# Background conversions of a fused attention and two-layer kernel: other places for the w_out halves, another order of the jobs, and earlier first sums

## The chip, the cores and the metric

The kernel runs on one core of a Trainium2 chip. The metric is the device time of one execution in microseconds (us). Engines are named as the profile names them: PE is TensorE (matmuls; PEld its weight loads), DVE is VectorE, ACT is ScalarE, POOL is GpSimd, SP is SyncE, which here only issues DMAs. Each engine works through its own queue in order and waits on semaphores for the others and for DMAs.

## The reference

What is computed, cut to what matters:

```
# attention: B=4, H=8, S=576, D=64; heads 0-3 local (32 back), 4-7 strided (every 32nd)
x  = softmax(mask(q @ k.T / 8)) @ v        # -> (2304 tokens, 512)
# layer 1
h  = x @ w_in1                             # (2304, 2048)
g  = s * relu(h)**2 + b
y  = g @ w_out1                            # (2304, 512)
# layer 2
h  = y @ w_in2
out = (h * cos(h)) @ w_out2
```

The weights reach the core as float64 words. They are turned into float32 on the chip.

## The kernel before, in words

**Arithmetic.** A float32 matmul is made of three fast ones: each operand is split into a high part (`split_hi`, L162, a copy on ACT into the type fp32r) and a low part (`split_lo`, L165, a subtraction on DVE), and PE forms hi·hi, lo·hi and hi·lo. `xhi` and `xlo` hold the activations, `gh` and `gl` those between w_in and w_out.

**Stages.** Attention comes first (until about 140 us, with slots beside it). Then, and partly beside it, come 40 *slots* (L881): one token block of up to 512 by one 128-wide slice of the hidden width, 30 slots for the first six slices, ten for two more. Slot 0 starts early; the last ends at 265.4 us. Then come 36 *units* (L1934): each does a pair of slices for 768 tokens with seven products of 2x2 blocks in place of eight, which need sums of blocks as operands, `xt`, `xdiff` (`run_forms1`, L1122) and sums of weight blocks. In a unit the products go to two banks `pa` and `pb`; ACT copies some out (`q<-pa`, L1946) and DVE adds a bank and a `q` into `h` (L1914). PE can write a bank again only after that. The w_out products of a unit (`triples`, L1814 and L1824) fill in between. Layer 2 begins at about 465 us, and its last part (`Blocks`, L1503 and L1633) at about 607 us.

**Background conversions.** While PE works through slots and units, the weights of the units to come are loaded, converted, split and stored in memory, and loaded again when the unit needs them (`wfl<-wfb`, `w2l<-w2s`). Such a job is a generator of single steps. A *pair* job (`pair_ops`): load 512 KB `praw` (L342), convert in place `ta` (L170 on ACT; L178, L179, L182 on DVE), four small sums `ts` (L355), three high splits (ACT), three low splits (DVE) into tiles `ob` and `oa`, three stores `wfb` (512 KB, L388), `wfa` (256 KB, L389), `wfc` (128 KB, L390). A *w_out* job (`out_ops`): load `oraw` (L395), convert in `tw` or in the spare end of q's tile, split into `ow`, store `w2s` (512 KB, L420). `ob`, `oa` and `ow` share the pool tag "v" with two places, so each new tile waits until the store of the tile two before has landed. `raw` tiles have two places as well.

**What sets the order.** The list `jobs2` gives the order of jobs: both halves of a pair, then both w_out tiles of it. How many steps go between two groups of matmuls stands in the tables `BG2` (by slot) and `BG2_UNIT` (by unit): a rate is added at each group, and whole steps are issued. So the steps stand at fixed points among the instructions of ACT, DVE and SP, and a step that waits holds what stands behind it on its engine. The conversion tiles come from pool "hs" (three places) up to slot 30, after it from "st" (four places). `run_forms1(0)` is started at slot 35 (`last == -5`) and gives one of its steps at each tick.

Of the kernel before, what the change touches and what calls it, by code (L numbers as in the profile page):

```python
# [9 lines left out]
F32 = mybir.dt.float32  # L10
F32R = mybir.dt.float32r
BF16 = mybir.dt.bfloat16
U32 = mybir.dt.uint32
AF = mybir.ActivationFunctionType
ALU = mybir.AluOpType
# [5 lines left out]
P = 128  # L21
# [7 lines left out]
KT = 64  # L29
LG, LK = 64, 96  # L30
# [50 lines left out]
HT = 384  # L81
# [25 lines left out]
LAST_USE = {"P2": 0, "P5": 1, "P3": 2, "P4": 3}  # L107
UNIT0 = ["P1", "P2", "t", "P6", "P5", "P7", "P3", "P4"]
UNIT = ["P1", "P2", "P6", "P5", "P7", "t", "P3", "P4"]
BG2 = ((15, 1.2), (18, 2.2), (22, 1.0), (30, 1.6), (36, 0.6), (38, 1.2))  # L110
BG2_UNIT = (1.2, 2.0, 2.0, 1.4, 1.4, 1.5, 1.5, 1.4, 1.6, 1.7, 1.7, 1.7, 1.4, 1.4, 1.4, 1.4, 1.4, 1.4, 1.4, 1.4, 1.6, 1.6)
NSUM = 6
ROOM = {10: (0, 2), 11: (0, 2), 12: (0, 2), 19: (1, 0), 20: (1, 1), 21: (0, 2), 22: (0, 2), 23: (1, 2), 24: (1, 1), 25: (0, 2), 26: (0, 2)}
OPERANDS = [(0, 0), (0, 1), (3, 1)]
MPLACES = [(5, 0), (4, 1)]
FORM_STEPS = (0, 0, 0, 3, 1, 1, 1, 3, 1, 1, 1, 3)
FORM_PACE = 4
TRIPLES = 12
TRIPLE_LAG = 2
LOADS = {  # L120
# [9 lines left out]
def net(ctx, tc, qkl, qks, rqk, vloc, vstr, rv, wi1, wo1, wp1, wo2, wp2, s, b, out):  # L130
    nc = tc.nc
# [16 lines left out]
    def psum(tag, name):  # L148
        return ps.tile([P, 512], F32, tag=tag, name=name, bufs={"h": 1, "acc": 4, "att": 3}[tag])

    ident = const.tile([P, P], F32, name="ident")
    identb = const.tile([P, P], BF16, name="identb")
    mloc = const.tile([P, 4, LK], BF16, name="mloc")
    mrem = const.tile([P, 4, KT], BF16, name="mrem")
    sb = const.tile([P, 32], F32, name="sb")
    xhi = const.tile([P, NC, NT], F32R, name="xhi")
    xlo = const.tile([P, NC, NT], F32R, name="xlo")
# [158 lines left out]
    def conv_tile(name):  # L316
        if plain_done[0]:
            return st_p.tile([P, 512], F32, tag="st", name=name)
        return h_p.tile([P, 512], F32, tag="hs", name=name)
# [76 lines left out]
        return raw  # L396

    def out_ops(raw, ly, n):
        t = whole = q0_tile()[:, HT:] if ly and n % 2 == 0 else conv_tile("tw")
        yield from to_f32(t, raw)  # L400
        bg2_load()
        if late:
            os = late_out(n % 2)
            t = t.rearrange("p (x c) -> p x c", x=2)
        else:
            o = io_p.tile([P, 2, 512], F32R, tag="v", name="ow")
            os = [o[:, h, :] for h in range(2)]
        apart = bool(late)
        yield lambda: split_hi(os[0], t)
        yield lambda: nc.sync.dma_start(out=w2f[n // 2][:, n % 2, :], in_=whole) if ly else None  # L410
        yield lambda: split_lo(os[1], t, os[0])
        yield lambda: None
        if apart:
            yield lambda: None
            for h in range(2):
                yield lambda h=h: nc.sync.dma_start(
                    out=w2s[ly, n][:, h, :].rearrange("p (x c) -> p x c", x=2), in_=os[h].bitcast(F32)
                )
        else:
            yield lambda: nc.sync.dma_start(out=w2s[ly, n], in_=o.bitcast(F32))  # L420
        stored2.add(("out", ly, n))

    def sum_load(p):
# [28 lines left out]

    jobs2 = []
    for ly, p in [(0, p) for p in range(PAIR1, NPAIR)] + [(1, p) for p in range(NPAIR)]:
        for m in range(2):
            jobs2.append((pair_load, pair_ops, (ly, p, m)))
        for f in range(2):
            jobs2.append((out_load, out_ops, (ly, 2 * p + f)))
    jobs2 += [(sum_load, sum_ops, (p,)) for p in range(NSUM)]
    gp = []  # L460
    loaded2 = []
# [2 lines left out]
    def q0_tile():  # L464
        if not qtile:
            qtile.append(rem_p.tile([P, HT + 512], F32, tag="rq", name="q0"))
        return qtile[0]
# [540 lines left out]
    early = 0  # L1008
# [116 lines left out]
    def new_temp(early):  # L1125
        return Temp(h_p.tile([P, 2, HT], F32, tag="hs", name="xt") if early else None)

    def split_temp(key, t):
        yield from free(key)
        hi, lo = place[key]  # L1130
        for m, src in t.ms:
            split_hi(hi[:, m], src)
        yield
        for m, src in t.ms:
            split_lo(lo[:, m], src, hi[:, m])
        formed.add(key)
        yield

    def run_forms1(s_):

        x11, x21, x12, x22 = (
            [x.bitcast(F32) for x in x_at(2 * s_ + half, kh)] for half in range(2) for kh in range(2)
        )
        key = {j: (0, s_, j) for j in range(2, 6)}
        early = s_ == 0
        t1, t2 = region_temps() if s_ == 2 else (new_temp(early), new_temp(early))
        yield from t1.set(x12[0], x12[1], ALU.add)
        for x in x11:
            yield from t1.set(t1, x)
        yield from t2.set(x22[0], t1)  # L1150
        yield from t2.set(t2, x22[1], ALU.add)
        if s_ < 2:
            yield from split_temp(key[3], t1)
        t4 = new_temp(early)
        yield from t4.set(x21[0], t2)
        yield from t4.set(t4, x21[1], ALU.add)
        yield from split_temp(key[2], t2)
        if s_ == 2:
            yield from split_temp(key[5], t4)
        for x in x11:  # L1160
            yield from t2.set(t2, x)
        if s_ == 2:
            yield from split_temp(key[3], t1)
        yield from split_temp(key[4], t2)
        if s_ < 2:
            yield from split_temp(key[5], t4)
# [140 lines left out]
    def region_temps():  # L1307
        return [Temp(x) for x in two(part_p.tile([P, RG], F32, tag="r21", name="xtemp"))]

    for t in range(NSLOT):  # L1310
        if t in W_AT:
            bg.append(lambda m=W_AT[t]: w_job(*m))
        for blk, need in ((1, 1), (2, 2), (3, 3)):
            if t == blk * FP:
                while not att.batch_done(need):
                    next(steps, None)
                    tick()
        last = t - NSLOT
        if t == 30:
            plain_done[0] = True  # L1320
        if last == -18:
            with tc.issue_after(relu[0].ins):
                nc.scalar.activation(sb[:, 4:5], sb[:, 3:4], AF.Sin)
        if last == -5:
            stages.append(run_forms1(0))
        if last == -3:
            spill(2)
        if last == -2:
            claim(2)
        if last == -1:  # L1330
            spill(1)
        for o, i in ((-9, 0), (-7, 1), (-5, 2), (-3, 3), (-2, 4), (-1, 5)):
            if last == o:
                load_wf(i)
        for o, i in ((-9, 0), (-8, 1), (-4, 2)):
            if last == o:
                load_w2(BUFS[i])
        first = t < FP
        for c in range(8):
            if c < 4 and (t, c) not in ((0, 0), (0, 1)):  # L1340
                mm_h(t, c)
            if c >= 4 and t >= LAG:
                mm_2(t - LAG, c - 4)
            tick()
            if c == 3:
                spawn(run_act(t))
            if c < 4 or t >= LAG:
                attention(RATE[min(t // FP, 2)])
            bg_step(BG0 if first or W_AT_FROM <= t < W_AT_TO else BG)
            for at, rate in BG2[::-1]:  # L1350
                if t >= at:
                    bg2_step(rate)
                    break
# [714 lines left out]
```

## Time and profile before

| | |
|---|---|
| median of 3 runs | 835.51 us (835.07 to 835.54) |
| the profiled execution | 833.12 us, span 831.3 us |
| PE busy | 817.1 us, 98% |
| DVE busy | 677.7 us, 82% |
| ACT busy | 585.5 us, 70% |
| granted TensorE clock | 1.00 (the 2.4 GHz level) |
| DMA | 220 MB, mean 265 GB/s |

The span is the time from the first to the last instruction of the profile; the execution's own time is 1.8 us longer. The profiled execution is 2.4 us below the median of the timed ones. PE is the engine to look at: where it stands idle, the time grows.

### The profile page before, as it was taken

The numbers are of one execution on the slowest core, as the hardware profiler recorded it, in microseconds if no ns is written. First come the engines' busy times: TensorE is split into PE (matmuls) and PEld (weight loads), VectorE is DVE, ScalarE is ACT, GpSimd is POOL, SyncE is SP. The second block draws the span as 40 slices with busy tenths as digits, with TensorE's granted clock in tenths as the row PEclk, the third lists the DMA queues.
The fourth block names the chain that finished last, engine by engine and source line by source line (L and its number), as shares of the span: only waits on it lengthen the run. The fifth ranks groups of instructions, "written<-read, shape, count | busy, mean of one in ns | idle before, by whom it ended". The sixth has DMA issues, their size and how long they took to land.

```text
span 831.3 us, 15491 instructions
## 1 busy us (share of the span) xinstructions
PE 817.1 (98%) x5545; PEld 731.7 (88%) x5545; DVE 677.7 (82%) x1294; ACT 585.5 (70%) x1232; POOL 20.5 (2%) x73
## 2 busy tenths in 40 slices
PE   8999999999999999999999999999999999999998
PEld 5677788788988899989989998899899999999998
DVE  6999665787998879996977698877758999578985
ACT  7888867768876787677678566557558765489753
POOL 3111000000000000000000000000000000000000
PEclk9999999999999999999999999999999999999999
DMA  9765433366989988887799989999798778874675
GB/s 338 237 190 166 135 105 92 122 248 227 324 318 343 366 324 285 313 290 267 264 346 371 295 281 345 318 311 383 255 358 264 269 249 253 290 259 152 205 250 179
DMA packets 101981, 220.00 MB, mean 265 GB/s; under 512 B 9104, under 2 KB 53392, under 8 KB 101904
## 3 DMA queue, kind: packets, MB, share of 16 engines
q1 hardware_dynamic: 100176, 211.83, 74.8%
q10 hardware_dynamic: 1728, 7.18, 2.4%
q8 instruction: 44, 0.72, 0.3%
q14 instruction: 33, 0.27, 0.1%
HBM read 163.92 MB, written 55.05 MB: 263 GB/s over the span
## 4 chain that ended last, share of the span: by engine, by line
PE 73%; DVE 13%; ACT 6%; DMA 6%; issue 2%; POOL 1%; ACTq 0%; POOLq 0%; DVEq 0%; SPq 0%
PE acc L1824 10%; PE acc L1633 9%; PE pb L1934 8%; PE pa L1934 8%; PE acc L1814 8%; PE h_ps L881 7%; PE acc L881 7%; PE acc L1503 5%; PE pa L1503 3%; PE pb L1503 3%; ACT part L623 2%; DVE xlo L165 1%; DVE graw L1095 1%; DMA praw<-in_wp_dram 1%; PE o_ps L695 1%
## 5 line engine op out<-in xcount | busy, mean ns | idle before, releaser
L881 PE MATMUL h_ps<-xhi,w 128*128 128x512 f32 (+1 forms) x320 | 101.8, 377 | 0.4 <-ACT w L162 0.4
L881 PE MATMUL acc<-gh,w 128*128 128x512 f32 (+1 forms) x320 | 100.6, 375 | 0.0
L1824 PE MATMUL acc<-gh,w2l 128*128 128x512 f32 (+1 forms) x384 | 84.6, 336 | 0.0
L1934 PE MATMUL pb<-xhi,wfl 128*128 128x384 f32 x268 | 80.0, 339 | 2.4 <-DVE h L1914 2.1
L1934 PE MATMUL pa<-xhi,wfl 128*128 128x384 f32 x268 | 79.7, 338 | 0.0
L162 ACT ACTIVATE xhi<-graw 128x384 fp32r<-128x384 f32 (+1 forms) x84 | 51.2, 629 | 38.4 <-DVE graw L1095 18.3
L881 PEld LDWEIGHTS h_ps<-xhi,w 128*128 128x128 f32 x320 | 58.4, 188 | 12.2 <-ACT w L162 1.0
L881 PEld LDWEIGHTS acc<-gh,w 128*128 128x128 f32 x320 | 58.3, 189 | 10.1 <-ACT gh L162 0.2
L1633 PE MATMUL acc<-xhi,w2m 128*128 128x384 f32 x256 | 67.1, 334 | 0.0
L1824 PEld LDWEIGHTS acc<-gh,w2l 128*128 128x128 f32 x384 | 60.1, 188 | 7.2
L165 DVE TENSOR_TENSOR xlo<-graw,xhi 128x384 fp32r<-128x384 f32 (+1 forms) x84 | 54.9, 685 | 7.5 <-ACT xhi L162 7.5
L1814 PE MATMUL acc<-w2l,gh 128*128 128x512 f32 x192 | 60.4, 390 | 0.0
L881 PE MATMUL acc<-gl,w 128*128 128x512 f32 (+1 forms) x160 | 59.8, 374 | 0.1
L881 PE MATMUL h_ps<-xlo,w 128*128 128x512 f32 (+1 forms) x160 | 59.4, 371 | 0.0
L1503 PE MATMUL acc<-xhi,wfl 128*128 128x384 f32 x196 | 55.4, 335 | 0.9 <-DMA wfl<-wfb 0.8
L1371 ACT ACTIVATE h<-h 128x768 f32<-128x768 f32 x48 | 40.4, 842 | 21.9 <-DVE h L1914 21.6
L1934 PEld LDWEIGHTS pb<-xhi,wfl 128*128 128x128 f32 x268 | 49.4, 188 | 5.4 <-DVE h L1914 3.0
L165 DVE TENSOR_TENSOR gl<-r,gh 128x512 fp32r<-128x512 f32 (+2 forms) x56 | 40.6, 725 | 14.7 <-ACT gh L1371 8.4
L1934 PEld LDWEIGHTS pa<-xhi,wfl 128*128 128x128 f32 x268 | 49.5, 188 | 1.8 <-DVE h L1914 0.4
L1824 PE MATMUL acc<-gl,w2l 128*128 128x512 f32 x192 | 49.9, 336 | 0.0
L1633 PEld LDWEIGHTS acc<-xhi,w2m 128*128 128x128 f32 x256 | 46.4, 188 | 0.0
L1934 PE MATMUL pa<-xlo,wfl 128*128 128x384 f32 x134 | 45.1, 336 | 0.0
(251 smaller groups left out, 2129.2 us busy)
## 6 DMA issues: line engine op xcount, KB each, us to landing
wfl<-wfb SPq DMA_DIRECT2D x68, 512.0 KB, 5.2
wfl<-wfa SPq DMA_DIRECT2D x34, 512.0 KB, 5.9
w2l<-w2s SPq DMA_DIRECT2D x28, 512.0 KB, 5.8
praw<-in_wp_dram SPq DMA_DIRECT2D x22, 512.0 KB, 4.3
oraw<-in_wo_dram SPq DMA_DIRECT2D x22, 512.0 KB, 5.3
w2m<-wsum SPq DMA_DIRECT2D x22, 512.0 KB, 4.2
wfb<-ob SPq DMA_DIRECT2D x21, 512.0 KB, 4.3
w2s<-ow SPq DMA_DIRECT2D x20, 512.0 KB, 5.1
```

Source lines behind the costliest of these rows:

```text
L162: nc.scalar.activation(dst_hi, src, AF.Copy)
L165: return nc.vector.tensor_tensor(dst_lo, src, hi.bitcast(F32), ALU.subtract)
L623: nc.scalar.activation(self.p[j][:, t, :], src[:, t, :], AF.Exp, bias=self.sm[j][:, 0, t : t + 1], scale=SCALE if self.pe_mask else 1.0, a ...
L695: prev = nc.tensor.matmul(o[b_][d, c : c + w], v[r, slot_, d], pt[r, q : q + w], start=True, stop=True)
L881: nc.tensor.matmul(*args, **kw)
L1095: return nc.vector.tensor_tensor(d, x, y, op)
L1371: return nc.scalar.activation(*args, **kw)
L1503: nc.tensor.matmul(self.bank(v, bi), a, b[:, m, :], start=st and m == 0 and i == 0, stop=m == 1 and i == 2, skip_group_check=True)
L1633: nc.tensor.matmul(self.acc(j, e), w[u][:, wi, c], g[:, u], start=first and i == 0, stop=last and i == 2, skip_group_check=True)
L1814: nc.tensor.matmul(accs[e], g[:, e * P : (e + 1) * P], w[:, wi, :], start=start and i == 0, stop=stop and i == 2, skip_group_check=True,)
L1824: nc.tensor.matmul(o, w[:, wi, e * P : (e + 1) * P], g[:, c : c + o.shape[1]], start=start and i == 0 and (c == 0 or e % 2 == 0), stop=sto ...
L1934: nc.tensor.matmul(pb[bi], a, b[:, m, :], start=st and m == 0 and i == 0, stop=m == 1 and i == 2, skip_group_check=True)
```

## The change

The four constants of attention (`ident`, `identb`, `mloc`, `mrem`) become views of one tile `consts` of 2 KB a partition. When attention is done, `consts` holds the high half of each w_out tile. The low half goes into the spare end of q's tile (`spare`), or, where that one holds the tile being converted (layer 2, even n), into a conversion tile `tl`. The tile `ow` of pool "v" is gone, and the store `w2s` is two DMAs of 256 KB instead of one of 512 KB. In `jobs2` a pair half and a w_out tile take turns. The sums of unit 0 start at slot 30 (`last == -10`) with three temporaries at once from pool "hs", and three pauses (`FORM_EARLY`) after each sum. The tables of rates are set anew; background steps before slot 18 are gone.

```diff
-BG2 = ((15, 1.2), (18, 2.2), (22, 1.0), (30, 1.6), (36, 0.6), (38, 1.2))
+BG2 = ((18, 2.4), (30, 0.6), (34, 0.3), (37, 0.4))
...
+FORM_EARLY = 3
...
-    ident = const.tile([P, P], F32, name="ident")
-    identb = const.tile([P, P], BF16, name="identb")
-    mloc = const.tile([P, 4, LK], BF16, name="mloc")
-    mrem = const.tile([P, 4, KT], BF16, name="mrem")
+    consts = const.tile([P, 512], F32, name="consts")
+    ident = consts[:, :P]
+    constb = consts[:, P:].bitcast(BF16)
+    identb = constb[:, :P]
+    mloc = constb[:, P : P + 4 * LK].rearrange("p (n k) -> p n k", n=4)
+    mrem = constb[:, P + 4 * LK :].rearrange("p (n k) -> p n k", n=4)
...
     def out_ops(raw, ly, n):
-        t = whole = q0_tile()[:, HT:] if ly and n % 2 == 0 else conv_tile("tw")
+        spare = q0_tile()[:, HT:]
+        t = whole = spare if ly and n % 2 == 0 else conv_tile("tw")
         yield from to_f32(t, raw)
...
         else:
-            o = io_p.tile([P, 2, 512], F32R, tag="v", name="ow")
-            os = [o[:, h, :] for h in range(2)]
+            assert att.done
+            low = conv_tile("tl") if ly and n % 2 == 0 else spare
+            os = [x.bitcast(F32R) for x in (consts, low)]
...
-            yield lambda: nc.sync.dma_start(out=w2s[ly, n], in_=o.bitcast(F32))
+            yield lambda: [nc.sync.dma_start(out=w2s[ly, n][:, h, :], in_=os[h].bitcast(F32)) for h in range(2)]
...
     jobs2 = []
     for ly, p in [(0, p) for p in range(PAIR1, NPAIR)] + [(1, p) for p in range(NPAIR)]:
-        for m in range(2):
-            jobs2.append((pair_load, pair_ops, (ly, p, m)))
-        for f in range(2):
-            jobs2.append((out_load, out_ops, (ly, 2 * p + f)))
+        for i in range(2):
+            jobs2.append((pair_load, pair_ops, (ly, p, i)))
+            jobs2.append((out_load, out_ops, (ly, 2 * p + i)))
...
         early = s_ == 0
+        if early:
+            t1, t2, t4 = (new_temp(True) for _ in range(3))
+            for t, x, y, op in (
+                (t1, x12[0], x12[1], ALU.add),
...
+                (t4, t4, x21[1], ALU.add),
+            ):
+                yield from t.set(x, y, op)
+                for _ in range(FORM_EARLY):
+                    yield
+            while key[2] not in place:
+                yield
+            yield from split_temp(key[2], t2)
+            yield from split_temp(key[3], t1)
+            for x in x11:
+                yield from t2.set(t2, x)
+            yield from split_temp(key[4], t2)
+            yield from split_temp(key[5], t4)
+            return
...
-        if last == -5:
+        if last == -10:
             stages.append(run_forms1(0))
```

Three places in the order of the instructions follow. Before, ACT's queue in the second unit, beside matmuls of about 280 to 288 us (line, operation, output and input tiles with their numbers, size):

```order
L1371 ACTIVATE h2_3814<-h2_3814 128x768 x2
L1946 ACTIVATE q0_3597<-pb_3779 128x384
L1382 ACTIVATE h2_3814<-h2_3814,sb_91 128x768
L162 ACTIVATE gh1_3907<-h2_3814 128x768
L1946 ACTIVATE q_3936<-pb_3779 128x384
L1371 ACTIVATE h2_3872<-h2_3872 128x768
L162 ACTIVATE ob_3921<-ts_3896 128x2x256
L170 ACTIVATE q0_3597<-oraw_3757 128x512
L162 ACTIVATE oa_3922<-ta_3859 128x256
L162 ACTIVATE oa_3922<-ta_3859 128x128
L1946 ACTIVATE q_3957<-pb_3779 128x384
```

The same place now (`split_hi` is L165 here, `rebias` L173, the copy of a bank L1973):

```order
L1398 ACTIVATE h2_3810<-h2_3810 128x768 x2
L1973 ACTIVATE q0_2593<-pb_3775 128x384
L1409 ACTIVATE h2_3810<-h2_3810,sb_88 128x768
L165 ACTIVATE gh1_3900<-h2_3810 128x768
L165 ACTIVATE consts_87<-q0_2593 128x512
L1973 ACTIVATE q_3929<-pb_3775 128x384
L1398 ACTIVATE h2_3868<-h2_3868 128x768
L173 ACTIVATE ta_3937<-praw_3755 128x512
L1973 ACTIVATE q_3950<-pb_3775 128x384
L1398 ACTIVATE h2_3868<-h2_3868 128x768
```

Between the two copies of bank `pb` stood a split of a pair and the first step of a w_out tile; now the first step of a pair stands there, and a w_out split ahead of both.

Before, ACT's queue beside matmuls of about 358 to 369 us:

```order
L1946 ACTIVATE q_4756<-pa_3778 128x384
L1371 ACTIVATE h2_4587<-h2_4587 128x768
L1382 ACTIVATE h2_4587<-h2_4587,sb_91 128x768
L162 ACTIVATE gh1_4786<-h2_4587 128x768
L162 ACTIVATE ow_4735<-q0_3597 128x512
L170 ACTIVATE ta_4833<-praw_4733 128x512
L162 ACTIVATE ow_4802<-tw_4776 128x512
L1371 ACTIVATE h2_4722<-h2_4722 128x768 x2
```

The same place now:

```order
L1973 ACTIVATE q_4750<-pa_3774 128x384
L165 ACTIVATE consts_87<-q0_2593 128x512
L1398 ACTIVATE h2_4580<-h2_4580 128x768
L173 ACTIVATE ta_4688<-praw_4513 128x512
L1409 ACTIVATE h2_4580<-h2_4580,sb_88 128x768
L165 ACTIVATE gh1_4779<-h2_4580 128x768
L173 ACTIVATE tw_4808<-oraw_4639 128x512
L1398 ACTIVATE h2_4717<-h2_4717 128x768
```

The two w_out splits are one, ahead of `gh1`; the first step of a pair moved ahead of `gh1` as well, and that of a w_out tile stands where the pair's stood.

Before, DVE's queue in slots 34 and 35, beside matmuls of about 250 to 259 us (`part<-acc` is the evacuation of a finished block, `gl` the low split that PE takes next):

```order
L165 TENSOR_TENSOR oa_3460<-ta_3424,oa_3460 128x128
L355 TENSOR_TENSOR ts_3521<-ta_3501 128x128 x2
L355 TENSOR_TENSOR ts_3521<-ts_3521,ta_3501 128x128
L165 TENSOR_TENSOR gl_3555<-r_3533,gh_3549 128x512
L355 TENSOR_TENSOR ts_3521<-ta_3501,ts_3521 128x128
L178 TENSOR_SCALAR q0_3597<-q0_3597 128x512
L179 SCALAR_TENSOR_TENSOR q0_3597<-oraw_3443,q0_3597 128x512
L165 TENSOR_TENSOR ob_3542<-ts_3521,ob_3542 128x2x256
L165 TENSOR_TENSOR oa_3543<-ta_3501,oa_3543 128x256
L165 TENSOR_TENSOR oa_3543<-ta_3501,oa_3543 128x128
L182 SCALAR_TENSOR_TENSOR q0_3597<-oraw_3443,q0_3597 128x512
L956 TENSOR_TENSOR part10_99<-acc_3592,part10_99 128x512
```

The same place now (`split_lo` is L168, `to_f32` L181, L182 and L185, `ts` L358, `Temp.set` L1126):

```order
L168 TENSOR_TENSOR tl_3316<-q0_2593,consts_87 128x512
L182 SCALAR_TENSOR_TENSOR ta_3360<-praw_3263,ta_3360 128x512
L1126 TENSOR_TENSOR xt_3323<-xhi_89,xt_3322 128x768
L185 SCALAR_TENSOR_TENSOR ta_3360<-praw_3263,ta_3360 128x512
L1126 TENSOR_TENSOR xt_3323<-xt_3323,xlo_90 128x768
L358 TENSOR_TENSOR ts_3403<-ta_3360 128x128 x2
L358 TENSOR_TENSOR ts_3403<-ts_3403,ta_3360 128x128
L1126 TENSOR_TENSOR xt_3324<-xhi_89,xt_3323 128x768
L358 TENSOR_TENSOR ts_3403<-ta_3360,ts_3403 128x128
L1126 TENSOR_TENSOR xt_3324<-xt_3324,xlo_90 128x768
L181 TENSOR_SCALAR tw_3550<-tw_3550 128x512
L168 TENSOR_TENSOR ob_3446<-ts_3403,ob_3446 128x2x256
```

Four sums `xt` stand here that stood after slot 35; `xt_3324` is the third temporary of pool "hs" after the tile `tl_3316` and has its place. `oa_3447` and `gl_3577`, of slot 35, follow in the next three rows.

## Rows read from the trace of the kernel before

**Rows 1.** The page, part 1: busy us, share of span, instructions.

```profile
PE 817.1 (98%) x5545; PEld 731.7 (88%) x5545; DVE 677.7 (82%) x1294; ACT 585.5 (70%) x1232; POOL 20.5 (2%) x73
```

**Rows 2.** Waits of PE, 150 to 610 us: total, times, longest.

```profile
PE pb L1934 <- DVE h L1914: 2.1, 2, 1.2
PE pb L1934 <- ACT q L1946: 1.1, 1, 1.1
PE acc L1503 <- DMA wfl<-wfb: 0.8, 1, 0.8
PE pa L1934 <- ACT q L1946: 0.5, 1, 0.5
PE pb L1934 <- DVE part L956: 0.3, 1, 0.3
```

**Rows 3.** Stretches: busy PE, PEld, DVE, ACT, POOL; clock, DMA share, GB/s.

```profile
240.00:265.00 25.00, 25.00 (x133) 21.54 (x132) 22.17 (x49) 17.50 (x33) 0.00 (x0) 1.00 0.88 328
265.00:290.00 25.00, 23.11 (x121) 20.43 (x120) 21.29 (x45) 17.52 (x30) 0.00 (x0) 1.00 1.01 380
```

**Rows 4.** Timeline, 277 to 288 us: start, us, engine, line, operation; idle before.

```profile
277.68 0.68 DVE L165 TENSOR_TENSOR ob<-ts,ob 128x512 fp32r<-128x512 f32 x1
278.71 0.39 SPq L388 DMA_DIRECT2D wfb<-ob  x1
285.29 0.63 ACT L162 ACTIVATE ob<-ts 128x512 fp32r<-128x512 f32 x1 [1.26 <-DMA wfb<-ob]
287.01 0.47 ACT L1946 ACTIVATE q<-pb 128x384 f32<-128x384 f32 x1
287.53 1.14 PE L1934 MATMUL pb<-xdiff,wfl 128*128 128x384 f32 x5 [1.10 <-ACT q L1946]
```

**Rows 5.** Waits of ACT for DMAs, 150 to 610 us.

```profile
ACT ta L170 <- DMA praw<-in_wp_dram: 6.3, 5, 2.7
ACT ob L162 <- DMA wfb<-ob: 3.1, 2, 1.9
ACT xdiff L162 <- DMA spilled<-part: 2.6, 2, 1.9
ACT oa L162 <- DMA wfc<-oa: 2.6, 3, 1.7
ACT tw L170 <- DMA oraw<-in_wo_dram: 1.8, 1, 1.8
ACT ow L162 <- DMA wfb<-ob: 1.5, 2, 1.1
```

**Rows 6.** Timeline, 361 to 369 us.

```profile
361.00 0.33 SPq L342 DMA_DIRECT2D praw<-in_wp_dram  x1
366.21 0.66 ACT L170 ACTIVATE ta<-praw 128x512 f32<-128x512 f32 x1 [2.67 <-DMA praw<-in_wp_dram]
368.58 0.45 PE L1934 MATMUL pb<-xhi,wfl 128*128 128x384 f32 x1 [0.87 <-DVE h L1914]
```

**Rows 7.** Timeline, 420 to 434 us.

```profile
420.03 0.33 SPq L395 DMA_DIRECT2D oraw<-in_wo_dram  x1
426.33 0.66 ACT L170 ACTIVATE tw<-oraw 128x512 f32<-128x512 f32 x1 [1.78 <-DMA oraw<-in_wo_dram]
433.01 0.44 PE L1934 MATMUL pb<-xhi,wfl 128*128 128x384 f32 x1 [1.25 <-DVE h L1914]
```

**Rows 8.** Groups of DVE, 250 to 265 us: busy us, mean ns.

```profile
L1122 DVE TENSOR_TENSOR xt<-xt,xhi 128x768 f32<-128x768 f32 x1 | 1.0, 957 | 0.0
L182 DVE SCALAR_TENSOR_TENSOR q<-oraw,q 128x512 uint32<-128x512 uint32 x1 | 0.7, 683 | 0.0
L355 DVE TENSOR_TENSOR ts<-ta 128x128 f32<-128x128 f32 x2 | 0.5, 281 | 0.0
```

**Rows 9.** The 21 stores of L389, `wfa<-oa`, 256 KB.

```profile
DMA to landing us min/median/max: 2.0/4.1/8.6
```

**Rows 10.** The 21 stores of L388, `wfb<-ob`, 512 KB.

```profile
DMA to landing us min/median/max: 2.7/4.3/8.4
```

More of the change, by code (lines that the diff above doesn't have):

```diff
@@ L109 @@
 UNIT = ["P1", "P2", "P6", "P5", "P7", "t", "P3", "P4"]
-BG2 = ((15, 1.2), (18, 2.2), (22, 1.0), (30, 1.6), (36, 0.6), (38, 1.2))
-BG2_UNIT = (1.2, 2.0, 2.0, 1.4, 1.4, 1.5, 1.5, 1.4, 1.6, 1.7, 1.7, 1.7, 1.4, 1.4, 1.4, 1.4, 1.4, 1.4, 1.4, 1.4, 1.6, 1.6)
+BG2 = ((18, 2.4), (30, 0.6), (34, 0.3), (37, 0.4))
+BG2_UNIT = (1.4, 1.6, 1.7, 1.5, 1.5, 1.5, 1.5, 1.5, 1.7, 1.7, 1.7, 1.7, 1.5, 1.5, 1.5, 1.5, 1.6, 1.6, 1.6, 1.6, 1.6, 1.6)
 NSUM = 6
@@ L1145, in run_forms1 @@
         early = s_ == 0
+        if early:
+            t1, t2, t4 = (new_temp(True) for _ in range(3))
+            for t, x, y, op in (
+                (t1, x12[0], x12[1], ALU.add),
+                (t1, t1, x11[0], ALU.subtract),
+                (t1, t1, x11[1], ALU.subtract),
+                (t2, x22[0], t1, ALU.subtract),
+                (t2, t2, x22[1], ALU.add),
+                (t4, x21[0], t2, ALU.subtract),
+                (t4, t4, x21[1], ALU.add),
[12 more added lines that the diff above has]
+            return
         t1, t2 = region_temps() if s_ == 2 else (new_temp(early), new_temp(early))
```

## The prediction, made before the changed kernel ran

> **What bounds the kernel now.** I read the page's busy shares first: TensorE (PE) works for 817.1 of the 831.3 us of the span, so at most 14.2 us can be won without taking matmuls away [rows 1]. The change takes none away: each engine has the same instructions before and after, apart from 20 DMA issues more on SP's queue. Next I read who PE waited for in the stretch the change touches, 150 to 610 us. There are six idle times: two for `h<-bank,q` of VectorE (DVE), together 2.1 us, 1.1 and 0.5 for `q<-bank` of ScalarE (ACT), 0.3 for `part<-acc`, and 0.8 for a weight load of the last stage [rows 2]. The first five add to 4.0 us; that is all a better deal of the background conversions can give back. The table by stretches puts 1.9 us of it into 265 to 290 us, where PE is busy 23.11 of 25 us at full granted clock and the DMA engines are full (share 1.01); from 240 to 265 us PE is never idle but DVE is busy 22.17 of 25 us [rows 3].
>
> Then I followed each idle time back in the timeline. The largest shows the pattern. At 278.71 SP issues the store `wfb<-ob` of the first half of a pair. ACT reaches `ob<-ts` of the second half, which takes the same place of pool "v", and stands 1.26 us, released at 285.29 by that store, 6.5 us after its issue. ACT works in order: `q<-pb` behind it runs only at 287.01, and PE, which wants the bank, stands 1.10 us [rows 4]. The others are alike: ACT held by a load or store that has not landed, an evacuation late behind it. The list of ACT's waits has all of them: `ta<-praw` 6.3 us in five waits, `ob` 3.1, `xdiff` on the spill 2.6, `oa` 2.6, `tw<-oraw` 1.8, `ow` 1.5 [rows 5]. That is 15 waits, 17.9 us, and five idle times of PE with 4.0 us: most of them fall where ACT has room. So the bound is PE, and the loss is the landing time of DMAs where ACT's queue has no slack.
>
> **The change part by part.** The sum is made against the profiled execution, 833.12 us (span 831.3 and 1.8 around it), which is 2.4 us below the median of the timed runs, 835.51; I carry the difference over.
>
> *Own places for w_out halves, pairs and w_out tiles in turn.* The high half goes to the old constants' place, the low half to the spare end of q's tile or to a conversion tile; pool "v" is left to `ob` and `oa`, and between the two halves of a pair stands a w_out job. At 282 us ACT's queue after the change reads `consts<-q`, `q`, `h`, `ta<-praw`, `q`, `h`; no `ob` is in front of the evacuation any more, and the store that `consts` waits for was issued a whole pair job earlier. So the 1.10 us go [rows 4]. Near 362 us ACT stood 2.67 us before `ta<-praw`, whose load was issued at 361.00; DVE's `h` came late and PE lost 0.87 us [rows 6]. After the change the pair conversion that stands there uses a load that stands earlier in SP's order, beside matmuls that PE ran at about 346 us, and the load issued near 360 feeds a `tw` that stands behind `gh`. I take the 0.87 us off. The 0.3 us before `pb` at 266 us comes from DVE being late since ACT waited 1.7 us for the store `wfc<-oa` of the other half of the same pair [rows 5]; in turn with w_out that wait goes: 0.32 off.
>
> *Two it touches only in part.* At 272 us ACT's `xdiff<-xt` waits up to 1.9 us for a spill of `part` to memory [rows 5], costing PE 0.5 us [rows 2]. The spill is issued in the same slot after the change, but the `q<-pa` that stood behind this `xdiff` stands ahead of it, while PE needs the `xdiff` itself soon after; I take half, 0.24 (bounds: all, and nothing). At 426 us `tw<-oraw` waits 1.78 us for a load issued at 420.03; PE loses 1.25 us at 433.01 [rows 7]. After the change a `tw<-oraw` stands near the same matmuls, its load no earlier, but the `q` and the `h` that followed it in ACT's queue stand ahead of it; half again, 0.63 (bounds: all, and nothing). Removed so far 1.10 + 0.87 + 0.32 + 0.24 + 0.63 = 3.16 us.
>
> *First sums from slot 30 on.* Seven sums and four splits that began in slot 35 now begin in slot 30, three temporaries at once. The last one takes, in a pool of three places, that of the tile `tl`, the low half of a w_out tile whose store has just been issued. On DVE stand between the split of `tl` and that sum two steps of `ta` of 0.683 us (by the same steps of `q`), two sums of 0.957 and three small sums of 0.281 [rows 8], together 4.1 us. SP issues a store 0.35 us after the split ends (278.71 against 277.68 + 0.68 [rows 4]), and the 256 KB store of the same shape, `wfa<-oa`, lands after 2.0 at least, 4.1 in the median, 8.6 at most [rows 9]. The wait is so 0.35 + 4.1 - 4.1 = 0.4 us in the median, nothing to 4.9 us at the ends. Behind it in DVE's queue stand the splits of a pair and then `gl` of slot 35, which PE takes at once; DVE has 2.8 us of room in these 25 us [rows 3], but none in this piece. I take 0.4, the value of the median row. A `tl` tile and a temporary meet like this a second time near 322 us, with over 6 us of sums between, so without a wait in the median.
>
> *More, smaller stores.* Twenty stores of 512 KB become forty of 256 KB. An issue holds SP about 0.39 us [rows 4], 20 of them 8 us in some 280 us, and SP is nowhere what PE waits for there [rows 2]. The row says that halving hardly shortens a landing: 4.1 us for 256 KB against 4.3 for 512 [rows 9, 10].
>
> The Trainium skill, "DMA: Bandwidth & Descriptors", section Anatomy of one DMA, gives each DMA a fixed cost of about 2 us plus its bytes over 436 GB/s, and the section Bandwidth asks for DMAs of 1 MiB and more; both speak against halving a store. By its fit, an estimate, a half would land in 2.6 us and a whole in 3.2, and the 0.4 us at `tl` would be nothing, the sum 0.4 us lower; the rows here are longer and nearly equal, so they agree with the fixed part and not with the rest.
>
> *New waits elsewhere.* Other work now meets the landings: ACT's `q<-oraw` at 347 and 382 us needs q's spare end, whose store was issued two or three us before; the low ends of landings give nothing, 8.6 us gives some 5 us of ACT. By the trace one DMA wait of ACT in three costs PE anything, 0.8 us each (4.0 us in five of 15) [rows 2, 5]. Two or three such waits make 2.5 x 0.8 / 3 = 0.7; I take 0.8, bounds 0 and 2.4.
>
> *At nothing.* The four constants become one tile: no instruction and no wait of the start moves. The 0.8 us of a weight load in the last stage [rows 2] hang on stores of that stage, whose order stays.
>
> Sum: -3.16 + 0.4 + 0.8 = -1.96. The profiled time becomes 831.2, the median 835.51 - 1.96 = 833.55; I write 833.5.
>
> **Rivals.**
> *All five idle times go and nothing comes.* For it: the causes in rows 4 to 7 are the same resource, and 10 of 15 waits of ACT already cost nothing. Against: the DMA engines stay full at 265 to 290 us with the same bytes. 835.51 - 4.0 = 831.5.
> *The waits move house.* The bytes, the loads and ACT's queue stay; landings of 4 to 8 us meet other rows, and five waits cost what five cost before. For it: the fourfold spread of landings [rows 9] and the DMA share of 0.88 to 1.01 [rows 3]. It gives 835.5, with 1 us either way.
> *The sum at slot 34 stops DVE.* Mechanism, place and price as above: `xt` waits for the store of `tl` while `gl` of slot 35 stands behind it. It decides from the point where the wait exceeds the 3.16 us removed, a landing of 3.16 + 4.1 - 0.35 = 6.9 us; by the longest, 8.6, DVE stands 4.9 us, and the time is 835.5 - 3.2 + 4.9 = 837.2; with only the half of the removed terms, 838.8. For it: 328 GB/s at 0.88 share in 240 to 265 us, and DVE already full [rows 3]. Against: the median row.
>
> **How the numbers follow.** A measurement of this kernel can tell 0.2%, 1.7 us, from no change. My forecast, between -0.8 and -3.2 us: 0.45. All gone, beyond -3.2: 0.14. Moved house, -0.8 to +1.7: 0.25. Slower by the stop: 0.16. Of the forecast's 0.45 about 0.32 lies beyond -1.7. Faster so 0.46, same 0.38, slower 0.16. The forecast's own range is 832.3 to 834.7. The range for 8 in 10 goes from 831.0 (a little past all gone) to 837.2 (the stop at its longest landing with the whole gain).
>
> **What would show it.** After the change PE's waits should have no `pb<-xdiff` for `q` near 286 us and none for `h` near 368; ACT's list no `ob` on `wfb<-ob` before an evacuation; `xt` of L1126 on DVE a wait for `w2s` of under 1 us near 255 us; SP's 256 KB stores of `consts` landing in about 4 us. I am wrong if PE stands at slot 35 for `gl`, if `ta<-praw` waits still add to 6 us, or if the sum of PE's waits in 150 to 610 us is above 4.8 us.

## The result, and the profile after

| | before | after |
|---|---|---|
| median of 6 runs | 835.29 us | 842.50 us |
| profiled span | 831.3 us | 841.0 us |
| PE busy | 817.1 us | 820.3 us |
| PE idle in the span | 14.2 us | 20.7 us |

The changed kernel is slower: the ratio of the times is 1.0086, with a 95% interval of 1.0073 to 1.0099, some 7 us. The forecast was 2 us faster, and the time lies outside the range. The ratios and intervals below leave out one execution of e11 (1137 us) and one of e12 (1614 us), which only their medians in the table count.

The page's busy shares, which answer to [rows 1]:

```profile
PE 820.3 (98%) x5545; PEld 734.2 (87%) x5545; DVE 678.8 (81%) x1294; ACT 585.0 (70%) x1232; POOL 20.6 (2%) x73
```

The span grew by 9.7 us: 6.5 of idle time on PE, and 3.2 of busy time for the same 5545 matmuls. Whom PE waited for from 150 to 610 us in the changed kernel (answers to [rows 2]; total, times, longest):

```profile
PE acc L885 <- ACT gh L165: 5.0, 1, 5.0
PE acc L885 <- DVE gl L168: 2.0, 3, 0.9
PE pb L1961 <- DVE h L1941: 1.7, 1, 1.7
PE pa L1961 <- DVE h L1941: 1.4, 2, 0.9
PE acc L1851 <- DMA w2l<-w2s: 0.3, 1, 0.3
```

None of the old rows for `q` or `part` is left: the idle times at 266, 273, 286 and 368 us are gone, 2.8 of the 4.0 us. The new rows add to 10.4 us, half of them in one piece. The stretches (answers to [rows 3]; busy PE, PEld, DVE, ACT, POOL, then clock, DMA share, GB/s) say where:

```profile
240.00:265.00 25.00, 20.14 (x100) 16.78 (x99) 19.95 (x42) 13.02 (x26) 0.00 (x0) 1.00 0.97 346
265.00:290.00 25.00, 24.19 (x117) 21.63 (x118) 22.59 (x43) 15.03 (x29) 0.00 (x0) 0.87 0.84 296
```

PE, never idle from 240 to 265 us before, loses 4.9 us there, and the granted clock behind it falls to 0.87 of full. The timeline of the changed kernel around that hole (start, us, engine, line, operation; idle before, releaser):

```profile
253.59 0.33 ACTq L1320 DMA_DIRECT2D spilled<-part  x1
254.18 0.32 SPq L425 DMA_DIRECT2D w2s<-tl  x1
259.46 0.84 ACT L165 ACTIVATE xdiff<-xt 128x768 fp32r<-128x768 f32 x1 [3.95 <-DMA spilled<-part]
262.45 0.96 DVE L1126 TENSOR_TENSOR xt<-xhi,xt 128x768 f32<-128x768 f32 x1 [4.75 <-DMA w2s<-tl]
263.64 0.63 ACT L165 ACTIVATE ob<-ts 128x512 fp32r<-128x512 f32 x1 [2.85 <-DVE ts L358]
264.69 0.40 ACT L165 ACTIVATE gh<-r 128x256 fp32r<-128x256 f32 x1
265.14 0.80 PE L885 MATMUL acc<-gh,w 128*128 128x256 f32 x2 [5.00 <-ACT gh L165]
266.61 0.79 PE L885 MATMUL acc<-gl,w 128*128 128x512 f32 x1 [0.67 <-DVE gl L168]
267.20 0.63 PE L885 MATMUL acc<-gh,w 128*128 128x512 f32 x1
267.63 0.63 PE L885 MATMUL acc<-gl,w 128*128 128x512 f32 x1
272.03 0.40 PE L885 MATMUL h_ps<-xhi,w 128*128 128x512 f32 x1
```

Read it from PE backwards. PE stands 5.00 us for `gh`. On ACT `gh` stands behind `ob<-ts`, which waits for DVE's last `ts`; on DVE that `ts` stands behind the sum `xt`, which waits 4.75 us until the store of `tl`, issued at 254.18, has landed: 8.3 us. ACT had lost 3.95 us of its own to a spill (the store of a `part` tile to memory, whose place `xdiff` takes) before that. Then the matmuls run at half speed: 0.43 us from one start to the next at 267 us, where 0.23 is usual, until 272 us. That is about 3.0 of the 3.2 us of busy time.

The fifth old idle time, 1.25 us at 433 [rows 7], is now 1.71 us at 441, with the same cause:

```profile
429.05 0.56 SPq L398 DMA_DIRECT2D oraw<-in_wo_dram  x1
436.36 0.66 ACT L173 ACTIVATE tw<-oraw 128x512 f32<-128x512 f32 x1 [1.73 <-DMA oraw<-in_wo_dram]
441.42 0.44 PE L1961 MATMUL pb<-xhi,wfl 128*128 128x384 f32 x1 [1.71 <-DVE h L1941]
```

The waits of ACT and DVE for DMAs (answers to [rows 5]; 150 to 620 us):

```profile
ACT tw L173 <- DMA oraw<-in_wo_dram: 4.5, 4, 1.7
ACT xhi L165 <- DMA w2s<-xhi: 4.3, 2, 3.0
ACT xdiff L165 <- DMA spilled<-part: 4.0, 1, 4.0
ACT q L173 <- DMA w2s<-q: 3.0, 3, 1.4
ACT ta L173 <- DMA praw<-in_wp_dram: 2.1, 3, 1.0
DVE xt L1126 <- DMA w2s<-tl: 4.7, 1, 4.7
```

The waits on `wfb` and nearly all on `wfc` have gone, and those for `praw` are a third. Those for `oraw` rose from 1.8 to 4.5 us. New are the waits for the stores of the new places, `w2s<-q` and `w2s<-tl`, and in layer 2 one on `w2s<-xhi`.

### The profile page after: what moved, and what is told of

It is laid out like the page before. It is cut to its first block, busy times and chain, and to the rows that moved or that the text cites. A ratio compares the mean times of both kernels' runs of the same rounds, so it can differ in the third digit from the quotient of the medians.

```text
span 841.0 us, 15549 instructions
## 1 busy us (share of the span) xinstructions
PE 820.3 (98%) x5545; PEld 734.2 (87%) x5545; DVE 678.8 (81%) x1294; ACT 585.0 (70%) x1232; POOL 20.6 (2%) x73
## 4 chain that ended last, share of the span: by engine, by line
PE 67%; DVE 15%; ACT 7%; DMA 7%; issue 2%; POOL 1%; SPq 0%; ACTq 0%; DVEq 0%; POOLq 0%
PE acc L1851 10%; PE pa L1961 8%; PE pb L1961 8%; PE acc L1660 7%; PE acc L885 6%; PE acc L1841 6%; PE h_ps L885 6%; PE acc L1530 5%; PE pa L1530 3%; PE pb L1530 2%; ACT part L627 2%; DVE graw L1099 2%; DMA praw<-in_wp_dram 2%; DVE xlo L168 2%; DMA w2s<-q 2%
## 5 line engine op out<-in xcount | busy, mean ns | idle before, releaser
L885 PE MATMUL acc<-gh,w 128*128 128x512 f32 (+1 forms) x320 | 102.7, 380 | 5.0 <-ACT gh L165 5.0
L165 ACT ACTIVATE xhi<-graw 128x384 fp32r<-128x384 f32 (+1 forms) x84 | 51.3, 630 | 38.4 <-DVE graw L1099 18.5
L168 DVE TENSOR_TENSOR xlo<-graw,xhi 128x384 fp32r<-128x384 f32 (+1 forms) x84 | 55.0, 687 | 7.7 <-ACT xhi L165 7.7
L1398 ACT ACTIVATE h<-h 128x768 f32<-128x768 f32 x48 | 40.3, 840 | 20.7 <-DVE h L1941 20.5
L168 DVE TENSOR_TENSOR gl<-r,gh 128x512 fp32r<-128x512 f32 (+2 forms) x56 | 40.6, 726 | 11.1 <-ACT gh L1398 6.6
L1961 PE MATMUL pb<-xlo,wfl 128*128 128x384 f32 x134 | 44.9, 335 | 0.0
```

Source lines behind the costliest of these rows:

```text
L165: nc.scalar.activation(dst_hi, src, AF.Copy)
L168: return nc.vector.tensor_tensor(dst_lo, src, hi.bitcast(F32), ALU.subtract)
L885: nc.tensor.matmul(*args, **kw)
L1398: return nc.scalar.activation(*args, **kw)
L1961: nc.tensor.matmul(pb[bi], a, b[:, m, :], start=st and m == 0 and i == 0, stop=m == 1 and i == 2, skip_group_check=True)
```

## The experiments

All at a glance; the ratio is to the kernel before, run on the same chip beside it.

```
run                          places turn sums at  rates by slot/unit  median   ratio  95% interval
changed kernel                 new   new   30       new / new         842.50  1.0086  1.0073-1.0099
e1  tiles from st at 29        new   new   30       new / new         841.52  1.0079  1.0057-1.0101
e2  sums at 35                 new   new   35       new / new         839.21  1.0045  1.0029-1.0060
e3  sums alone                 old   old   30       old / old         834.92  0.9995  0.9981-1.0010
e4  turn alone                 old   new   35       old / old         836.12  1.0013  0.9997-1.0030
e5  rates alone                old   old   35       new / new         844.54  1.0120  1.0081-1.0158
e6  places and turn            new   new   35       fewer / old       838.51  1.0045  1.0027-1.0063
e7  places alone               new   old   35       old / old         836.41  1.0016  1.0001-1.0030
e8  first tl in v              new   new   30       new / new         844.73  1.0117  1.0100-1.0134
e9  old rates                  new   new   30       old* / old        837.21  1.0023  1.0002-1.0043
e10 old rates by slot          new   new   30       old* / new        840.33  1.0062  1.0039-1.0086
e11 places and turn, old rates new   new   35       old* / old        836.24  1.0009  0.9995-1.0023
e12 the same, new by unit      new   new   35       old* / new        839.49  1.0055  1.0035-1.0074
e13 gl first                   new   new   30       new / new         839.14  1.0040  1.0021-1.0060
e14 gl first, tl in v          new   new   30       new / new         837.72  1.0025  1.0000-1.0051
e15 old rates by unit          new   new   30       new / old         841.80  1.0074  1.0050-1.0098
e16 e14 and old by unit        new   new   30       new / old         837.75  1.0031  1.0019-1.0043
old*: from slot 17 in place of 15, and 1.3 in place of 1.0 in slots 22 to 29
```

**e1, the tile `tl` out of the temporaries' pool.**

```diff
-        if t == 30:
+        if t == 29:
             plain_done[0] = True
```

> The changed kernel, but conversion tiles come from pool st one slot earlier (from slot 29), so the tile tl of the first layer-2 w_out job no longer has the place that the third temporary xt takes. Theory 1 (the 5.0 us idle time of PE at slot 35, the 0.7 behind it and the 3.2 us of slow clock after it come from DVE's xt waiting 4.7 us for the store of tl): that wait is gone, PE has no idle time over 1 us between 240 and 265 us, and the time falls by 7 to 9 us from 842.5 to 833 to 835.5. Theory 2 (it is ACT's xdiff, which waits 4.0 us for the spill because the sums are ready before the spill is issued): the wait for the spill stays at 3 to 5 us, PE loses 2 to 5 us there, time 838 to 842. Theory 3 (the new places and the deal of the jobs cost the time): 840 or more.

841.5 us: theory 1 missed in this form, and theory 2's spill was not it either (1.2 us at most). The time is also one that theory 3 gave. PE has a new hole of 6.2 us, ahead of the old one. Its rows:

```profile
243.79 0.68 ACT L173 ACTIVATE q<-oraw 128x512 f32<-128x512 f32 x1 [3.59 <-DMA w2s<-q]
250.95 0.68 DVE L168 TENSOR_TENSOR gl<-r,gh 128x512 fp32r<-128x512 f32 x1
251.69 0.80 PE L885 MATMUL acc<-gl,w 128*128 128x512 f32 x1 [6.20 <-DVE gl L168]
```

`gh` was ready at 240.2 us, but DVE, busy without a gap, came to `gl` at 250.95: the sums, no longer held by a tile, stood ahead of it, with the conversions. Taking one wait away let the order of DVE's queue change.

**e2, the sums as before.** The new branch of `run_forms1` is out, and the start is at slot 35 again.

```diff
-        if last == -10:
+        if last == -5:
             stages.append(run_forms1(0))
```

> The changed kernel with the first unit's sums as before: started at slot 35, third temporary made late. Places, order of jobs and rates as changed. Theory 1 and theory 2: neither wait exists in this form, PE has no idle time over 1 us between 240 and 265 us, the time is 832.5 to 835.5. Theory 3: it stays at 840 or more.

839.2: between the theories. The stop is gone, 3.4 us with it by the ratios, and 4 us stay. Two of PE's waits make up most of them, one behind `tw<-oraw` near 436 us, one behind the spill:

```profile
PE pb L1938 <- DVE h L1918: 3.2, 2, 2.9
PE pa L1938 <- ACT xdiff L165: 1.6, 1, 1.6
```

**e3, the early sums alone.** The new branch and `last == -10` in the kernel before.

> The kernel before with nothing changed but the sums from slot 30 on with three temporaries at once. There is no tile tl in it. Theory 1: no long wait of DVE for a store, 834 to 837. Theory 2: ACT's xdiff waits 3 us or more for the spill and PE loses 2 to 5 us at slots 35 to 36, 837 to 841. Theory 3: 835.

834.9, no change: early sums without the new deal of the jobs do no harm, and theory 2 does not hold for them.

**e4, the turn alone.**

```diff
-        for m in range(2):
-            jobs2.append((pair_load, pair_ops, (ly, p, m)))
-        for f in range(2):
-            jobs2.append((out_load, out_ops, (ly, 2 * p + f)))
+        for i in range(2):
+            jobs2.append((pair_load, pair_ops, (ly, p, i)))
+            jobs2.append((out_load, out_ops, (ly, 2 * p + i)))
```

> The kernel before with nothing changed but the order of the jobs: a pair half and a w_out tile in turn, all of them still in pool v. All theories for the loss: no change there, 833 to 836. For the five small idle times: if the order of jobs alone takes them away, their sum in 260 to 440 us falls from 4.0 to under 2 us and the time to 832.5 to 834; if the own places are needed, ob still waits for stores (over 2 us in sum) and the time stays within 1 us of 835.3.

836.1, not told from before. The pairs' waits on `wfb` go, but `oa` now waits 11.0 us in sum for `w2s<-ow`, and one idle time of 3.0 us (`pb`, for `part`) takes the place of three. Without the own places the turn moves the waits.

**e5, the tables of rates alone.**

> The kernel before with the new tables of rates alone; places, order and sums as before. Theory R (the rates cost what is left in the run with sums at slot 35, 4 us: background work starts at slot 18 with 2.4 steps a group, DVE falls behind and gl comes late): 837.5 to 840. Theory P (the places cost it, each w_out job waits for the store of the one before it): 834 to 836.

844.5, more than theory R gave: the rates, put into the old kernel, cost 10 us (7 to 13 by the interval). `ow` and `ob` wait 9.7 us for `wfb`, and PE for `gl`:

```profile
PE acc L881 <- DVE gl L165: 5.6, 2, 3.3
```

**e6, places and turn, at old rates from slot 17.**

> The kernel before with the new places and the jobs in turn, at the old rates (background work from slot 17 in place of 15, as attention must be done before the constants' place is reused); sums as before. Theory R: 832.5 to 835.5, the five small idle times of PE mostly gone. Theory P: 837 to 840, with waits of ACT for w2s<-q or w2s<-consts of 3 us or more.

838.5, above what theory R gave, but not by theory P's waits: ACT has none for `w2s`. Between 260 and 440 us only two idle times are left, 0.48 and 1.17 us. Most of the loss is one wait at the start of the last stage, with the granted clock at 0.52 from 610 to 617 us; a wait of 1.48 us at 498 us is new too. 19 fewer steps by slot 40 (two slots of eight groups at 1.2) made SP issue the load later, at 605.46 in place of 601.66 us; e11, which has the steps back, stands 0.86 us there:

```profile
605.46 1.68 SPq L1220 DMA_DIRECT2D wfl<-wfb  x2
612.42 0.66 PE L1506 MATMUL acc<-xhi,wfl 128*128 128x384 f32 x1 [4.83 <-DMA wfl<-wfb]
```

**e7, the places alone.** The new `out_ops` and `consts` in the kernel before.

> The kernel before with the new places alone: order of jobs and rates as before, so both w_out tiles of a pair follow each other into the same place. Theory R: 834 to 837. Theory P: 838 to 842, with waits of ACT or DVE for w2s stores of 5 us or more, more than in the run with jobs in turn.

836.4: as theory R has it. By themselves the places cost 1.3 us, at most 2.5 by the interval, far from the 7.

**e8, the first `tl` in pool "v".**

```diff
-            low = conv_tile("tl") if ly and n % 2 == 0 else spare
+            low = (io_p.tile([P, 512], F32, tag="v", name="tl") if n == 0 else conv_tile("tl")) if ly and n % 2 == 0 else spare
```

> The changed kernel with one edit: the first tl (layer 2, n = 0) lies in pool v, not in the pool of the temporaries. Theory 1 as it stood (the wait of xt for the store is what costs): no wait of xt on DVE, no idle time over 1 us at slots 34 to 36, 836 to 839.5 (what the run with sums at slot 35 has). Theory 1b (DVE has no room for the sums between slots 30 and 35 with this deal, and in the order gl stands behind them): the wait of xt is gone, but PE stands 3 to 7 us for gl between 240 and 265 us, time 840 to 843.

844.7: `xt` waits no more, and PE waits for `gl` instead, as theory 1b has it, though the time is above its 843:

```profile
PE acc L885 <- DVE gl L168: 6.0, 3, 4.6
```

In the order of the changed kernel `gl` of slot 34 stands ahead of the last sums, here behind them. So e1 and e8 each changed two things, and the cause stayed open until e13.

**e9 to e12, sums by rates.** Old rates by slot (17 and 1.3, so that the sum of steps is the old one), with the old or the new table by unit.

```diff
-BG2 = ((18, 2.4), (30, 0.6), (34, 0.3), (37, 0.4))
+BG2 = ((17, 1.2), (18, 2.2), (22, 1.3), (30, 1.6), (36, 0.6), (38, 1.2))
```

> The changed kernel (places, turn, sums from slot 30) with both tables of rates as before, but for background work from slot 17 in place of 15 and 1.3 in place of 1.0 in slots 22 to 29, so that the number of steps by the end of the slots is the old one. Theory R (the table of rates by slot is what makes the change slow: too many steps before slot 30 and too few after): no idle time over 1 us of PE between 200 and 270 us, 832 to 835.5. Theory S (sums from slot 30 on need room that the places and the turn do not leave): PE stands 2 us or more for gl or xdiff near slots 34 to 36, 837 to 841.

> As the run before, but with the new table of rates by unit. If only the table by slot does harm: within 1 us of the run before, 832 to 836. If the new table by unit does harm too (ACT's tw waits for its load near 435 us, PE 1.7 to 3 us): 2 us or more above it.

> Places and turn on the kernel before, old sums, old rates but for slot 17 in place of 15 and 1.3 in place of 1.0 in slots 22 to 29. Theory R: without the late wfl load of 4.8 us at 607 us that the earlier run with fewer steps had, and with the small idle times of PE between 260 and 440 us under 1.5 us in sum, 832.5 to 834.5. Rival: the waits move to other rows, 834.5 to 836.5.

> As the run before with the new table by unit. Differs from the run with sums at slot 35 only in the table by slot. Theory R: 832.5 to 836, at least 3 us below that run's 839.2. If it stays above 838, the table by unit costs the rest.

Old table by unit: 837.2 and 836.2; new: 840.3 and 839.5. Beside the old table by slot the new one by unit costs 3 us, with early or late sums; e9's and e10's difference alone is not clear of its intervals, e11's and e12's is. e9 is above theory R's range and has neither theory's sign: PE's longest idle time between 240 and 350 us is 0.63 us, but at 235 us it stands 1.56 us for `part`. Early sums cost about 1 us here, within the intervals; in e9 `tl` is made at 258.5 us, after the sums that would wait for its place. e12 against e2, 839.5 and 839.2: with late sums the new table by slot costs nothing, so theory R's 3 us are not there. e11 is not told from the kernel before, and its rival was the better guess: the small idle times moved to other rows (1.18 us at 272, 1.84 at 356). What the table by unit does is mostly one wait; e12 first, then e11:

```profile
424.98 0.37 SPq L397 DMA_DIRECT2D oraw<-in_wo_dram  x1
433.39 0.66 ACT L172 ACTIVATE tw<-oraw 128x512 f32<-128x512 f32 x1 [3.54 <-DMA oraw<-in_wo_dram]
439.09 0.44 PE L1937 MATMUL pb<-xhi,wfl 128*128 128x384 f32 x1 [3.45 <-DVE h L1917]
```

```profile
423.25 0.34 SPq L397 DMA_DIRECT2D oraw<-in_wo_dram  x1
429.93 0.66 ACT L172 ACTIVATE tw<-oraw 128x512 f32<-128x512 f32 x1 [0.66 <-DMA oraw<-in_wo_dram]
435.64 0.45 PE L1937 MATMUL pb<-xhi,wfl 128*128 128x384 f32 x1 [0.56 <-DVE h L1917]
```

The load lands 8.4 us after its issue in e12, 6.7 in e11, and is wanted about 5 and 6 us after it. Behind its hole e12 has the granted clock at 0.51 from 440 to 443.5 us; e11 has it at full.

**e13 and e14, the wait against the order.** `gl` of slots 30 to 39 is put first on DVE; e14 has the first `tl` in pool "v" besides, as e8. Both have the same order on DVE, all 435 instructions from 150 to 398 us.

```diff
-        split_lo(gl, r, gh)
+        with tc.high_priority() if t >= 30 else nullcontext():
+            split_lo(gl, r, gh)
         g_t[t] = (gh, gl)
```

> The changed kernel with gl of slots 30 to 39 put ahead of the sums on DVE; xt still waits for the store of tl. If the order of gl is the cause: no idle time over 1.5 us of PE between 240 and 270 us, 838 to 840. If the wait is the cause wherever gl stands: xt still waits 3 us or more, the next gl or xdiff behind it comes late, PE stands 2 us or more, 840.5 to 843.

> The same order on DVE, and the first tl in pool v, so that xt has no store to wait for. If the wait is the cause: 2.5 us or more below the run with gl first alone, 837 to 839.5, no idle time over 1.5 us of PE there. If the order is: equal to the run with gl first. If neither: an idle time of 3 us or more stays, with the spill in front of ACT's xdiff as the next suspect.

839.1 and 837.7. Two things were expected of e13, and both hold in part: the time falls by 3.4 us, clear of the intervals, though DVE's wait is as long as before and PE still loses 3.08 us. From e13:

```profile
262.38 0.96 DVE L1127 TENSOR_TENSOR xt<-xhi,xt 128x768 f32<-128x768 f32 x1 [4.72 <-DMA w2s<-tl]
264.45 0.42 DVE L168 TENSOR_TENSOR gl<-r,gh 128x256 fp32r<-128x256 f32 x1
264.92 0.39 PE L885 MATMUL acc<-gl,w 128*128 128x256 f32 x1 [3.08 <-DVE gl L168]
```

And from e14, where the sum has no store to wait for:

```profile
257.75 0.95 DVE L1127 TENSOR_TENSOR xt<-xhi,xt 128x768 f32<-128x768 f32 x1
262.74 0.43 DVE L168 TENSOR_TENSOR gl<-r,gh 128x256 fp32r<-128x256 f32 x1 [2.83 <-ACT gh L165]
```

The 3.08 us are gone. At that place PE waits 0.58 us for ACT's `gh`, although ACT has just waited 6.01 us for its spill:

```profile
260.80 0.85 ACT L165 ACTIVATE xdiff<-xt 128x768 fp32r<-128x768 f32 x1 [6.01 <-DMA spilled<-part]
262.76 0.38 PE L885 MATMUL acc<-gh,w 128*128 128x256 f32 x1 [0.58 <-ACT gh L165]
```

So in this order the traces show that the wait for the store makes the hole. The times do not tell e13 from e14: the medians differ by 1.4 us with overlapping intervals, where 2.5 were expected. The profile of e14 is of its slowest execution (840.72 us, against a median of 837.72), so its later waits, such as 2.64 us behind `q` at 282 us where e13 has 1.12, need not be those of the median. And e8 has a hole of 4.6 us without any wait of DVE ahead of it, where the order has `gl` behind the sums: wait and order can each stop PE here. Mending both takes 842.5 to 837.7, 5 of the 7 us, clear of the intervals.

**e15 and e16, the table by unit in the changed kernel.**

> The changed kernel with the old table of rates by unit; the table by slot, the places, the turn and the sums as changed. If the table by unit adds 3 us wherever it is used: 839 to 840, no idle time over 1 us near 441 us, the stop at slots 34 to 36 as before. If it only did harm beside the old table by slot: 841.5 to 843.

> The changed kernel with gl first, the first tl in pool v and the old table by unit. If these are the causes: 834 to 837. If a third one is left: 838 or more, with an idle time of PE over 2 us in 200 to 300 us.

841.8 against 842.5, and 837.75 against 837.72: beside the new table by slot the one by unit costs nothing that can be told. The 3 us of e9 to e12 do not add; they hang on where one load lands. e16's time falls between its two expectations, and no idle time of PE there is over 2 us. e16 is still 2.6 us (1.6 to 3.6) above the kernel before, so these causes are not all. A suspect is the spill, for which ACT waits in e16:

```profile
259.51 0.85 ACT L165 ACTIVATE xdiff<-xt 128x768 fp32r<-128x768 f32 x1 [4.83 <-DMA spilled<-part]
```

ACT comes to this `xdiff` at 254.7 us, 2.7 us after the spill was issued (251.96); in the kernel before, 9.3 us lay between the first spill and the `xdiff`. But the trace gives the spill little of PE's time: the next idle times of PE are 0.61 us at 267 and 0.65 at 271. The others are spread, and the one at 280 us stands behind a new place again, as ACT's `q<-oraw` has waited 2.46 us for `w2s<-q`. PE's waits of e16 from 150 to 610 us:

```profile
PE acc L1852 <- DMA w2l<-w2s: 1.6, 1, 1.6
PE acc L885 <- DVE gl L168: 1.6, 2, 1.0
PE pb L1962 <- ACT q L1974: 1.3, 1, 1.3
PE pa L1962 <- ACT q L1974: 1.3, 1, 1.3
PE pb L1962 <- DVE part L961: 0.6, 1, 0.6
```

With two smaller ones they add to 6.9 us, where the kernel before has 4.8. The loss that is left is thus several small waits at new rows, and which edit brings each stays open. Moving the `xdiff` alone was not tried. No run beat the kernel before.

## Why the prediction was wrong

*What held.* The five idle times were seen rightly and so was their cause; four of them are gone, those priced in full (1.10, 0.87, 0.32) and, beyond the half taken, the 0.47. The halved stores cost little, as the rows said: the `w2s` halves landed after 2.7 us at least, 5.3 in the median and 8.4 at most, and the 20 whole `w2s` stores of the kernel before (L420) took as long:

```profile
DMA to landing us min/median/max: 2.6/5.1/9.6
```

One tile for the constants cost the start nothing: PE is busy 134.46 us of the first 140 before and 134.44 after.

*The step that failed* is the one on the first sums: "I take 0.4, the value of the median row." The mechanism stood there, with its place (the sum `xt` behind the store of `tl`, ahead of the split of slot 35), and its upper end, 4.9 us, was what came: 4.75. The size was taken from the median of 21 landings [rows 9] over the whole conversion, where 240 to 265 us has the DMA engines 0.88 full before and 0.97 after. That row is also of another store; the one of the `w2s` store itself, above, would have given 0.35 + 5.1 - 4.1 = 1.4 us in the median. In the three profiles that have this wait (the changed kernel, e13, e15), the store, issued at 254.2 to 254.4 us, landed after 7.9 to 8.3 us, and `xt` waited 4.75, 4.72 and 4.42 us. At the second meeting of a `tl` tile and a temporary, near 325 us, only e1 and e2 have a wait, 1.43 and 0.33 us. The fit that the prediction takes from the Trainium skill, "DMA: Bandwidth & Descriptors", section Anatomy of one DMA, is given there for DMAs issued from GpSimd; these are issued by SP, and no run here tests it. The rival that was given 0.16 was the case, at a higher price than its own. Two of the three signs of being wrong came: PE stood at slot 35, for `gh` and then `gl`, and its waits add to 10.4 us; those of ACT for `praw` did not (2.1 us).

*What the rival's own price lacked.* It counted DVE's wait alone. In the trace the hole has three parts: 5.0 us, because ACT's `gh` hung on the same sum by way of `ts` and `ob`; 0.7 us more for `gl`; and 3.2 us more of busy time, nearly all of it matmuls at the lower clock after it. That makes 8.9 in place of 4.9. With PE's other waits, 1.7 + 1.4 + 1.3 + 0.3 (`h`, `gl` at two other places, `w2l`), and less the 4.0 of the kernel before, it is 9.6 of the 9.7 us by which the span grew. The range ended at 837.2 since the rival's price was 4.9.

*The 0.63 taken for 433 us* went the other way, by 0.46 us. `q` and `h` do stand ahead of `tw` there, but the next `h` behind it is as late as before. e11 and e12 show how far such a wait swings (0.56 and 3.45 us) by 1 or 2 us of a load's place and landing.

*The new waits elsewhere*, priced at 0.8 by one wait in three, are the second term that failed. Without the stop the forecast left PE 0.84 of the old 4.0 us and 0.8 of new waits. The changed kernel has 4.7 us beside the hole, and e16, where the hole is mended, 6.9: its time is 2.6 us above the kernel before, where the sum without the stop gave 2.4 below. That is the second rival, the waits that move house, on top of the stop.

## What to carry to other kernels

Where a wait for a DMA is new in an engine's queue, price it by the landing times of that stretch, and by their upper end where the DMA engines are full; then follow who stands behind it on every engine, not on one. A hole of several us on TensorE can cost more than its length, as here the matmuls behind it ran at the lower clock. Taking one wait away in a queue that something else orders moves the rest: change the order and the wait apart (e13, e14) before calling either the cause, and take a profile whose time is near the run's median.

## What the runs showed of the hardware

After a hole of 5.0 us TensorE's granted clock was 0.57 of full in the mean from 264 to 272 us; matmuls of 512 columns started 0.43 us apart, at the 1.2 GHz level, where they start 0.23 us apart at 2.4 GHz, and the trace has them back at the upper level at 272 us. Smaller idle times, up to 1.71 us in the same trace, left no such mark. In the other profiles the granted clock also fell to the lower level at holes of 6.20 us (e1), 4.83 (e6), 4.73 (e15), 4.64 (e8), 3.45 (e12) and 3.08 (e13), and at one of 1.98 us (e5, at 624 us), but not at one of 2.95 us (e2, at 439 us). The Trainium skill, "TensorE: Matmul & The Clock Gate", section on the clock gate, has the same two levels and start-to-start times of 426.7 and 215.7 ns for 512 columns; the trace agrees at the lower level (427 ns from 267.2 to 269.8 us) and is 5% above it at the upper (227 ns from 257.7 to 259.8 us). Loads and stores of 256 and 512 KB landed after 2.7 to 9.6 us in the changed kernel, and size hardly showed: the median of `wfa<-oa` (256 KB) and that of `wfb<-ob` (512 KB) were both 4.5 us.
